# Block sums for both products of the second MoE, and sums between SBUF buffers on Pool

## The chip, the cores and the metric

The kernel runs on one core of a Trainium2 chip. The metric is the device time of one execution in microseconds. Engines are named as in the profile: PE (TensorE; PEld is its weight load), DVE (VectorE), ACT (ScalarE), POOL (GpSimd), SP (SyncE).

## What is computed

Three stages stand in a row: attention with a position bias, a first MoE that takes the largest of three products, and a second MoE with a gate.

```python
def _attn_ref(q, k, v, w1, b1, w2):
    ...
    scores = scores + bias.transpose(2, 0, 1)[None, :, :, :]
    ...
    return np.matmul(attn, v).astype(np.float32)

def _moe_ref(x, w1, w2, w3, w_out):
    h = np.maximum(np.maximum(x @ w1, x @ w2), x @ w3)
    return (h @ w_out).astype(np.float32)

def _moe2_ref(x, w_gate, w_val, w_out):
    gate = 1.0 / (1.0 + np.exp(-(x @ w_gate)))
    val = x @ w_val
    return (gate * val @ w_out).astype(np.float32)
```

Attention has 4 batches, 8 heads, 576 positions and 64 features a head. The MoEs see 2304 tokens of 512 features; the first has 768 inner columns and the second 1536.

## The kernel before

Every fp32 operand is split into two f16 halves (`hi` and `lo`), and a product is three matmuls for each 128 rows of the contraction: hi·hi, hi·lo, lo·hi. `halves` (line 1100) makes such a pair: ACT writes the scaled `hi`, DVE subtracts it from the scaled source and writes `lo`.

**The second MoE** works on one batch of 576 tokens after another. `quad(b, i)` makes 256 of the 1536 inner columns for batch b: six quads a batch, 24 in all. Its gate product is done by Strassen's scheme in Winograd's form: tokens and weights are cut in 2 x 2 blocks, seven sums of blocks are multiplied (seven groups of six matmuls of 128x288 each) and added up into four blocks of the result. DVE does this adding (lines 1279 to 1287), with one operand from PSUM and one from SBUF. The value product is plain: eight groups of six matmuls, left in two double PSUM banks (`two_r`). That makes 90 matmuls for a quad. ACT takes the gate's sigmoid (line 1298), DVE multiplies it with the value straight out of PSUM (line 1300), ACT casts the product to `hi` (line 1306), and DVE subtracts (`add2`, line 1096) to get `lo`.

**The block sums of the operands.** `token_sums(b, ...)` reads a batch's tokens back from DRAM, makes four sums (`add2`) and puts eight blocks into `XC`, which has two buffers, so the next batch's blocks can be made while the last one's are read (`next_tokens`). `pair_weights(i, ...)` makes the weights of a quad: DMA of 64-bit numbers, `decode64` (lines 554 to 556, integer steps on DVE), a sum of squares on ACT, a column sum on PE, then the scaled blocks; for the gate four `add2` sums come first. `out_weights(c, ...)` does the same for a quarter of the output weights, with the column scale at line 1208.

**Output matmuls.** `outs(pr, ct)` multiplies 128 finished tokens of batch pair `pr` with the output weights: 36 matmuls of 128x512 into bank 7 (later bank 4 too). The tables `after` and `ends` say behind which quads which of them are written: from quad (1,0) on, they stand between the quads.

**What sets the order.** All operations are recorded (`Recorder`), and `emit` deals them out to the engines by class and by modelled start time. The result is one fixed queue for each engine. An engine that waits for a semaphore holds everything behind it in its queue. `nc.join()` offers several engines for the same operation; `ADD_POOL`, which is off, would do that for `add2`.

Of the kernel before, what the change touches and what calls it, by code (L numbers as in the profile page):

```python
# [453 lines left out]
def tile_kernel(ctx, tc, q, k, v, w1, b1, w2, mw1, mw2, mw3, mwo, gw, vw, ow, xtab, masks, out):  # L454
# [725 lines left out]
    ob_m = X2[:, 3968:4992]  # L1180
# [3 lines left out]
    sg_r = Ring([sg_f, X2[:, 2816:3968]])  # L1184
# [68 lines left out]
    part_r, two_r = Ring([bank(i)[:, 0:HS] for i in (5, 6)]), Ring([bank(i, 1024).rearrange("p (a s) -> p a s", a=2)[:, :, 0:HS] for i in (0, 2)])  # L1253
    RAW = ((0, 1), (7, 2))

    def quad(b, i):
# [3 lines left out]
        sg, XC = sg_r(), XC_[b % 2]  # L1260
        c21, c22, c11, c12 = (sg[:, HS * n:HS * (n + 1)] for n in range(4))
# [3 lines left out]
        def group(ps, W, o, x, start, stop):  # L1265
            with nc.join():
                for kk in range(2):
                    for z, (wp, xp) in enumerate(((0, 0), (0, 1), (1, 0))):
                        nc.tensor.matmul(ps, lhsT=W[:, o, wp, kk], rhs=XC[:, x, xp, kk], start=start and kk == z == 0, stop=stop and kk == 1 and z == 2)  # L1269

        vs = []
        for t, n in enumerate((1, 6, 7, 5, 2, 3, 4)):
            ps = part_r()
            group(ps, SW[i][0], WS[n - 1], n - 1, True, True)
            with nc.at(BIAS):
                if n == 1:
                    copy_psum(c11, ps)
                elif n == 6:
                    nc.vector.tensor_tensor(c12, ps, c11, op=ALU.add)
                elif n == 7:  # L1280
                    nc.vector.tensor_tensor(c21, ps, c12, op=ALU.add)
                elif n == 5:
                    nc.vector.tensor_tensor(c12, ps, c12, op=ALU.add)
                    nc.vector.tensor_tensor(c22, ps, c21, op=ALU.add)
                else:
                    c = {2: c11, 3: c12, 4: c21}[n]
                    nc.vector.tensor_tensor(c, ps, c, op=ALU.add)  # L1287
            if t in (0, 2, 3, 5):
                m, hf = ((1, 0), (1, 1), (0, 0), (0, 1))[(0, 2, 3, 5).index(t)]
                if not hf:  # L1290
                    pv = two_r()
                    vs.append((m, pv))
                for kh in range(2):
                    group(pv[:, hf], SW[i][1], 2 * m + kh, RAW[hf][kh], kh == 0, kh == 1)
        with nc.at(BIAS):
            for m, pv in vs:
                at = sg[:, S * m:S * m + S]
                nc.scalar.activation(at, at, AF.Sigmoid, scale=ugm)  # L1298
                at = at.rearrange("p (a s) -> p a s", a=2)
# [69 lines left out]
    tx = [X2[:, 4992:5568], X2[:, 5568:6144]]

    def next_tokens(b):
        with nc.at(ATT):
            gx = gm_f[(1, 0, 1)[b]]
            token_sums(b + 1, gx[:, 0:1152], gx[:, 3072:4224], tx[b % 2])

    next_tokens(0)
# [47 lines left out]
```

## Time and profile before

| what | value |
|---|---|
| median of 3 runs | 1039.08 us (1037.2 to 1039.49) |
| the profiled execution's own time | 1040.86 us |
| span of its trace | 1039.1 us |
| granted PE clock, mean | 0.993 |
| PE busy | 993.7 us, 96% |
| DVE busy | 722.9 us, 70% |
| ACT busy | 597.6 us, 58% |
| POOL busy | 120.0 us, 12% |

The profile is one execution. Its page gives busy time by engine, the chain of work that ended last, and groups of instructions by line with their mean duration and with the idle time before them. The trace answers narrower questions: busy time in any stretch, an engine's timeline, the same groups with shapes kept apart. A line number there is one of the kernel printed above.

### The profile page before, as it was taken

The page shows a single profiled execution, that of the slowest core. Times are in us where ns is not written, and L with a number is a line of the kernel's source. Part 1 is how long each engine was busy: PE and PEld are TensorE (multiplying, and loading weights), DVE is VectorE, ACT ScalarE, POOL GpSimd, SP SyncE. Part 2 cuts the span into 40 slices and gives each one's busy share as a digit, 9 for nine tenths or more (in the row PEclk, how much of TensorE's full clock was granted, in tenths as well). Part 3 has the DMA queues.
Part 4 walks back from the last instruction along what each step waited for, and adds up shares of the span by engine and source line. Part 5 has one row for each costly group of instructions (what it writes and reads, how often), then busy time and mean ns, then how long its engine had stood idle before and what let it go on. Part 6 is the DMA issues. An engine that isn't in the chain of part 4 may idle for free.

```text
span 1039.1 us, 21298 instructions
## 1 busy us (share of the span) xinstructions
PE 993.7 (96%) x8156; PEld 670.1 (64%) x8156; DVE 722.9 (70%) x1869; ACT 597.6 (58%) x1336; POOL 120.0 (12%) x146
## 2 busy tenths in 40 slices
PE   4898999997999999999999999999999999999998
PEld 2344577664666666677677777876666656766653
DVE  5788998976878789958779989996354335532320
ACT  6898986775787777856765565653233124222221
POOL 1022114342112322112100100000000000000000
PEclk9999999998999999999999999999999999999999
DMA  7896767567999999875686233420010001000001
GB/s 222 252 303 226 271 211 174 164 165 143 213 228 261 234 219 250 206 199 128 146 181 188 82 104 116 138 62 11 11 67 11 11 11 66 2 11 22 11 11 41
DMA packets 172242, 139.49 MB, mean 134 GB/s; under 512 B 111852, under 2 KB 151020, under 8 KB 171628
## 3 DMA queue, kind: packets, MB, share of 16 engines
q1 hardware_dynamic: 169476, 128.39, 47.6%
q10 hardware_dynamic: 2664, 9.74, 3.3%
q8 instruction: 64, 1.05, 0.4%
q14 instruction: 38, 0.31, 0.1%
HBM read 94.25 MB, written 21.23 MB: 111 GB/s over the span
## 4 chain that ended last, share of the span: by engine, by line
PE 77%; DVE 9%; DMA 3%; issue 2%; ACT 2%; POOL 2%; SPq 0%; ACTq 0%; POOLq 0%; DVEq 0%
PE ps L1269 22%; PE ps L945 19%; PE ps L1325 13%; PE ps L890 7%; PE ps L831 5%; PE ps L863 5%; DMA am<-am 2%; PE ps L834 2%; PE ps L669 2%; POOL am L858 1%; DVE am L1103 1%; DVE am L847 1%; DVE wm L975 1%; PE ps L566 1%; PE ps L611 1%
## 5 line engine op out<-in xcount | busy, mean ns | idle before, releaser
L945 PE MATMUL ps<-wm 128*128 128x320 f16 (+2 forms) x2304 | 304.9, 286 | 0.2 <-DVE am L975 0.2
L945 PEld LDWEIGHTS <-wm 128*128 128x128 f16 x2304 | 222.9, 99 | 54.9 <-issue 3.2
L1269 PE MATMUL ps<-am 128*128 128x288 f16 x1800 | 223.9, 286 | 1.3 <-DVE wm L1300 0.7
L1269 PEld LDWEIGHTS <-am 128*128 128x128 f16 x1800 | 176.1, 98 | 48.5 <-issue 1.6
L1325 PE MATMUL ps<-wm 128*128 128x512 f16 x648 | 142.5, 379 | 0.0
L848 ACT ACTIVATE am<-am,small 128x576 f32<-128x576 f32 (+1 forms) x160 | 123.1, 770 | 30.3 <-DVE small L847 19.4
L847 DVE CUSTOM_DVE_ANT_0 am<-ps,am 128x576 f32<-128x576 f32 (+1 forms) x160 | 117.9, 749 | 28.2 <-issue 13.0
L1325 PEld LDWEIGHTS <-wm 128*128 128x128 f16 x648 | 63.3, 98 | 73.5
L858 POOL TENSOR_SCALAR am<-am,small 128x576 f32<-128x576 f32 (+1 forms) x65 | 64.5, 997 | 206.1 <-DVE small L850 135.5
L890 PE MATMUL ps<-am 128*64 128x128 f32 (+4 forms) x980 | 81.0, 313 | 1.1 <-DVE wm L896 0.7
L592 ACT ACTIVATE am<-ps 128x512 f32<-128x512 f32 (+3 forms) x146 | 66.1, 472 | 26.9 <-PE ps L863 23.5
L863 PE MATMUL ps<-ident,am 128*128 128x128 f32 x450 | 72.2, 282 | 7.5 <-POOL am L858 6.1
L863 PEld LDWEIGHTS ps<-ident,am 128*128 128x128 f32 x450 | 51.1, 143 | 26.1 <-POOL am L858 10.4
L1298 ACT ACTIVATE x<-x,ug 128x576 f32<-128x576 f32 x24 | 18.6, 775 | 77.8 <-DVE x L1287 77.7
L831 PE MATMUL ps<-am 64*128 64x512 f16 (+1 forms) x390 | 55.1, 384 | 7.3 <-DMA am<-am 6.8
L1333 ACT ACTIVATE x<-ps,uo 128x128 f32<-128x128 f32 x64 | 18.2, 368 | 75.3 <-PE ps L1325 55.4
L1298 ACT ACTIVATE wm<-wm,ug 128x576 f32<-128x576 f32 x24 | 18.5, 771 | 56.8 <-DVE wm L1287 56.8
L890 PEld LDWEIGHTS ps<-am 128*64 128x64 f32 x680 | 39.5, 137 | 17.8 <-issue 4.9
L872 DVE SCALAR_TENSOR_TENSOR am<-am,small 128x576 f16<-128x576 f32 (+1 forms) x60 | 48.0, 825 | 3.9 <-ACT am L871 3.8
L975 DVE SCALAR_TENSOR_TENSOR wm<-ps,small,wm 128x256 f32<-128x256 f32 (+1 forms) x84 | 43.0, 512 | 8.5 <-PE ps L945 6.8
L1269 PE MATMUL ps<-am,x 128*128 128x288 f16 x360 | 46.0, 286 | 2.5 <-DVE am L1103 1.9
L871 ACT ACTIVATE am<-am,small 128x576 f16<-128x576 f32 (+1 forms) x60 | 43.6, 766 | 5.3 <-ACT am L848 2.7
(180 smaller groups left out, 1382.6 us busy)
## 6 DMA issues: line engine op xcount, KB each, us to landing
am<-bias_d SPq DMA_DIRECT2D x49, 576.0 KB, 4.6
bias_d<-am SPq DMA_DIRECT2D x36, 320.0 KB, 4.4
wm<-in_moe_w_dram SPq DMA_DIRECT2D x12, 768.0 KB, 6.2
am<-bias_d ACTq DMA_DIRECT2D x15, 576.0 KB, 4.9
wm<-in_moe_w_out_dram SPq DMA_DIRECT2D x24, 256.0 KB, 2.9
x<-in_moe_w_val_dram SPq DMA_DIRECT2D x20, 256.0 KB, 4.1
x_d<-wm SPq DMA_DIRECT2D x4, 1152.0 KB, 4.7
am<-in_v_dram SPq DMA_DIRECT2D x16, 256.0 KB, 5.7
```

The lines of the kernel that those rows point to most:

```text
L592: nc.scalar.activation(dst, src, AF.Copy, scale=scale)
L831: nc.tensor.matmul(s_main[o][:m], lhsT=q_[h, eq], rhs=k_[h, ek, 0:512], start=(i == 0), stop=(i == 2), tile_position=(64 * o, 0))
L847: nc.vector.tensor_tensor_reduce(e[:m, c], S_[o][:m], bt[:m, c], -1.0, 3.0e38, ALU.add, ALU.min, mx[:m])
L848: nc.scalar.activation(e[:m, c], e[:m, c], AF.Exp, scale=-1.0, bias=mx[:m], accum_out=l[:m, o:o + 1])
L858: nc.gpsimd.tensor_scalar(e[:m, c], e[:m, c], r[:m, o:o + 1], 1.0, op0=ALU.mult, op1=ALU.mult)
L863: nc.tensor.transpose(ps[:, t], e[:, 128 * (t0 + t):128 * (t0 + t) + 128], ident)
L872: nc.vector.scalar_tensor_tensor(ph[:m, 1, c], e[:m, c], f, ph[:m, 0, c], op0=ALU.mult, op1=ALU.subtract)
L890: nc.tensor.matmul(ps[64 * o:64 * o + 64, :N], lhsT=vv[:, o, tv], rhs=pp[:, tb], start=(i == j == 0), stop=(i == len(todo) - 1 and j == 4) ...
L945: nc.tensor.matmul(ps, lhsT=W(wp, kk), rhs=X(xp, kk), start=(first and i == 0), stop=(last and i == 2))
L975: nc.vector.scalar_tensor_tensor(hv, ps, f, hv, op0=ALU.mult, op1=ALU.max)
L1269: nc.tensor.matmul(ps, lhsT=W[:, o, wp, kk], rhs=XC[:, x, xp, kk], start=start and kk == z == 0, stop=stop and kk == 1 and z == 2)
L1325: nc.tensor.matmul(po, lhsT=g[:, gi, kk], rhs=OW[:, wi, kk], start=(kk == 0 and i == 0), stop=(kk == K2 - 1 and i == 2))
```

## The change

The value product gets the same seven groups as the gate. A quad now makes its 14 groups in turn (gate, value, gate, ...), 84 matmuls in all, and every group lies in a single PSUM bank from a ring of six. The value's blocks are added up by DVE in SBUF (buffers from a new ring, `rp_r`), and the multiplication of gate and value (line 1291 of the changed kernel) reads both from SBUF.

The value's weights get four block sums and seven blocks, as the gate's have. `XC` holds seven blocks and only one batch: `token_sums(b + 1)` is written behind the quads of batch b.

`add2` is issued by Pool alone. It makes the sums of weight blocks (256 elements a row) and of token blocks (576). The `lo` half of the quads' products (1024 elements a row) is Pool's for batches 0 and 1 (`LO_POOL = 2`) and DVE's for batches 2 and 3; the two tails of 64 tokens stay on DVE. The `outs` are written at other places.

```diff
-ADD_POOL = False
+ADD_POOL = True
+LO_POOL = 2
...
-        with nc.join():
-            nc.vector.tensor_tensor(dst, a, b, op=op)
-            if ADD_POOL:
-                nc.gpsimd.tensor_tensor(dst, a, b, op=op)
+        (nc.gpsimd if ADD_POOL else nc.vector).tensor_tensor(dst, a, b, op=op)
...
-            W, s = SW[i][j], scl_gv[:, 0, i, j:j + 1]
-            if j:
-                for h in range(2):
-                    halves([W[:, 2 * h:2 * h + 2, e] for e in range(2)], f[:, :, 128 * h:128 * h + 128].rearrange("p (o k) f -> p o k f", o=2), s)
-                    yield
-                continue
-            t = S4().rearrange("p (o k f) -> p o k f", o=4, k=2)
+            W, s, t = SW[i][j], scl_gv[:, 0, i, j:j + 1], S4().rearrange("p (o k f) -> p o k f", o=4, k=2)
...
-    XC_ = [Am[:, 14080 + 4608 * i:18688 + 4608 * i].bitcast(F16).rearrange("p (o e k s) -> p o e k s", o=8, e=2, k=2) for i in range(2)]
+    XC = Am[:, 17920:21952].bitcast(F16).rearrange("p (o e k s) -> p o e k s", o=7, e=2, k=2)
...
-    part_r, two_r = Ring([bank(i)[:, 0:HS] for i in (5, 6)]), Ring([bank(i, 1024).rearrange("p (a s) -> p a s", a=2)[:, :, 0:HS] for i in (0, 2)])
-    RAW = ((0, 1), (7, 2))
+    part_r = Ring([bank(i)[:, 0:HS] for i in (0, 1, 2, 3, 5, 6)])
...
+        for n in (1, 6, 7, 5, 2, 3, 4):
+            for j in range(2):
+                c21, c22, c11, c12 = C[j]
+                ps = part(n, j)
+                with nc.at(BIAS):
+                    if n == 1:
+                        copy_psum(c11, ps)
+                    elif n == 6:
+                        nc.vector.tensor_tensor(c12, ps, c11, op=ALU.add)
...
-                nc.vector.scalar_tensor_tensor(at, pv, DOWN2, at, op0=ALU.mult, op1=ALU.mult)
+                nc.vector.scalar_tensor_tensor(sg[:, at], (r0, r1)[m], DOWN2, sg[:, at], op0=ALU.mult, op1=ALU.mult)
...
-                add2(lo, src, hi, ALU.subtract)
+                (nc.gpsimd if LO_POOL > b and src.shape[2] > 64 else nc.vector).tensor_tensor(lo, src, hi, op=ALU.subtract)
...
-    after = {0: {}, 1: {0: [0], 1: [1], 2: [2], 3: [3]}, 2: {0: [5], 1: [6], 2: [7], 3: [8]}, 3: {0: [0], 1: [1], 2: [2], 3: [3]}}
-    ends = {0: [], 1: [4], 2: [], 3: [4, 5, 6, 7, 8]}
...
+    after = {0: {}, 1: {1: [2], 3: [3]}, 2: {0: [6], 2: [7], 3: [8]}, 3: {1: [2], 3: [3]}}
+    ends = {0: [0, 1], 1: [4, 5], 2: [0, 1], 3: [4, 5, 6, 7, 8]}
...
+        if b < B - 1:
+            with nc.at(BIAS):
+                gx = gm_f[(1, 0, 1)[b]]
+                token_sums(b + 1, gx[:, 0:1152], gx[:, 3072:4224], gx[:, 1152:1728] if b else ob_m[:, 0:576])
```

How the queues change is read from the order of the instructions. Buffers there are `am`, `wm` and `x_75` (three large SBUF buffers) and `ps` (PSUM); the brackets name the engines or DMA lanes whose semaphores an instruction waits for.

PE, where the output matmuls first come. Before, behind all of quad (1,0) and 66 matmuls of quad (1,1):

```order
L1269 MATMUL ps<-am 128x288
L1269 LDWEIGHTS am
L1269 MATMUL ps<-am 128x288
L1325 LDWEIGHTS wm
L1325 MATMUL ps<-wm 128x512 [waits Activation_49]
L1325 LDWEIGHTS wm
L1325 MATMUL ps<-wm 128x512 [waits DVE_49]
```

In the changed kernel they come behind all quads of batches 0 and 1 but for 24 matmuls, and behind the column sum (line 567) of the last quarter of the output weights:

```order
L1261 MATMUL ps<-am 128x288
L1261 LDWEIGHTS am
L1261 MATMUL ps<-am 128x288
L567 MATMUL ps<-small,ones 128x6 [waits Activation_49]
L1316 LDWEIGHTS wm
L1316 MATMUL ps<-wm 128x512 [waits Activation_49]
L1316 LDWEIGHTS wm
L1316 MATMUL ps<-wm 128x512 [waits DVE_49]
L1316 LDWEIGHTS wm [waits Pool_49]
```

So 984 quad matmuls now stand ahead of the first output matmul, where 696 stood, and that one waits for DVE's, ACT's and Pool's share.

DVE in one of batch 0's quads. Before, with the decoding of output weights in between:

```order
L1281 TENSOR_TENSOR wm<-ps,wm 128x288 [waits DVE_49,PE_49]
L555 SCALAR_TENSOR_TENSOR wm<-wm 128x256 [waits DVE_49]
L554 TENSOR_SCALAR wm<-wm 128x256 [waits DMAHW5_49]
L556 SCALAR_TENSOR_TENSOR wm<-wm 128x256 [waits DVE_49]
L1283 TENSOR_TENSOR wm<-ps,wm 128x288 [waits PE_49]
L1284 TENSOR_TENSOR wm<-ps,wm 128x288
```

The same place in the changed kernel:

```order
L1275 TENSOR_TENSOR wm<-ps,wm 128x288 [waits DVE_49,PE_49]
L1275 TENSOR_TENSOR x_75<-ps,x_75 128x288 [waits DVE_49,PE_49]
L1101 SCALAR_TENSOR_TENSOR wm<-wm,small 128x2x128 [waits Activation_49]
L1282 TENSOR_TENSOR wm<-ps,wm 128x288 [waits DVE_49,PE_49]
L1283 TENSOR_TENSOR wm<-ps,wm 128x288
L1282 TENSOR_TENSOR x_75<-ps,x_75 128x288 [waits DVE_49,PE_49]
L1283 TENSOR_TENSOR x_75<-ps,x_75 128x288
```

Each sum out of PSUM now stands there twice, for the gate and for the value.

Pool behind the weights' sums, in batches 0 and 1, in the changed kernel (before, Pool had nothing at all to do here):

```order
L1096 TENSOR_TENSOR wm<-wm 128x2x288 [waits Pool_49]
L1298 TENSOR_TENSOR wm<-wm 128x1024 [waits PE_49,Activation_49]
L1298 TENSOR_TENSOR wm<-x_75,wm 128x1024 [waits PE_49,Activation_49]
L1298 TENSOR_TENSOR wm<-wm 128x1024 [waits PE_49,Activation_49]
L1298 TENSOR_TENSOR wm<-x_75,wm 128x1024 [waits Activation_49]
L1096 TENSOR_TENSOR wm<-wm 128x2x288 [waits DVE_49,Pool_49]
L1298 TENSOR_TENSOR wm<-wm 128x1024 [waits PE_49,Activation_49]
L1096 TENSOR_TENSOR wm<-wm 128x2x288 [waits DVE_49,Pool_49]
```

The low halves (line 1298) and the sums of the second batch's tokens (line 1096, 2x288) share one queue.

## Rows read from the trace of the kernel before

**Rows 1.** The page's first part: busy time, share and instructions of each engine.
```profile
PE 993.7 (96%) x8156; PEld 670.1 (64%) x8156; DVE 722.9 (70%) x1869; ACT 597.6 (58%) x1336; POOL 120.0 (12%) x146
```

**Rows 2.** Busy time in stretches of 20 us: PE, PEld, DVE, ACT, POOL, clock, DMA.
```profile
680.00:700.00 20.00, 17.84 (x146) 14.00 (x146) 19.90 (x49) 11.63 (x26) 0.00 (x0) 1.00 0.17 53
```

**Rows 3.** The same view of two longer stretches.
```profile
535.66:710.56 174.90, 168.44 (x1366) 132.70 (x1365) 162.75 (x443) 104.41 (x251) 5.00 (x3) 1.00 0.35 109
...
707.11:1034.50 327.39, 327.39 (x2181) 212.94 (x2179) 129.33 (x257) 87.60 (x179) 0.00 (x0) 1.00 0.06 22
```

**Rows 4.** PE's timeline: start, duration, line, tile, count, [idle before, releaser].
```profile
623.97 2.37 PE L1269 MATMUL ps<-am,x 128*128 128x288 f16 x18
...
694.47 3.22 PE L1269 MATMUL ps<-am,x 128*128 128x288 f16 x25 [0.26 <-DVE x L1300]
699.59 3.93 PE L1269 MATMUL ps<-am,x 128*128 128x288 f16 x29 [1.90 <-DVE am L1103]
703.86 1.82 PE L1269 MATMUL ps<-am,x 128*128 128x288 f16 x12 [0.34 <-DVE wm L1281]
706.23 0.90 PE L1269 MATMUL ps<-am 128*128 128x288 f16 x6 [0.55 <-DVE wm L1287]
```

**Rows 5.** The chain that ended last: start, duration, engine, line, count.
```profile
752.62 11.03 PE ps L1269 x90
763.65 7.77 PE ps L1325 x36
...
1028.02 6.62 issue
```

**Rows 6.** DVE's timeline in a quad of batch 1.
```profile
713.18 0.46 DVE L1283 TENSOR_TENSOR x<-ps,x 128x288 f32<-128x288 f32 x1
713.56 0.45 DVE L1284 TENSOR_TENSOR x<-ps,x 128x288 f32<-128x288 f32 x1
```

**Rows 7.** Groups by line and shape: count, busy us, mean ns, idle before.
```profile
L1300 DVE SCALAR_TENSOR_TENSOR wm<-ps,wm 128x576 f32<-128x576 f32 x24 | 18.1, 756 | 13.5 <-ACT wm L1298 13.4
L1287 DVE TENSOR_TENSOR wm<-ps,wm 128x288 f32<-128x288 f32 x36 | 16.4, 454 | 9.7 <-PE ps L1269 8.8
L1096 DVE TENSOR_TENSOR wm<-wm 128x1024 f16<-128x1024 f32 x12 | 14.6, 1220 | 6.0 <-ACT wm L1306 6.0
L1103 DVE SCALAR_TENSOR_TENSOR wm<-wm,small 128x256 f16<-128x256 f32 x24 | 10.3, 476 | 0.0
L1096 DVE TENSOR_TENSOR am<-am 128x256 f32<-128x256 f32 x16 | 6.0, 412 | 0.0
L1103 DVE SCALAR_TENSOR_TENSOR am<-am,gv_su 128x1024 f16<-128x1024 f32 x4 | 5.1, 1276 | 0.0
L1103 DVE SCALAR_TENSOR_TENSOR am<-am,gv_su 128x512 f16<-128x512 f32 x4 | 3.0, 750 | 0.1
```

**Rows 8.** POOL's timeline, its last three instructions before the quads.
```profile
560.20 1.28 POOL L986 TENSOR_TENSOR wm<-wm 128x576 f16<-128x576 f32 x1 [52.49 <-ACT wm L984]
578.57 1.69 POOL L986 TENSOR_TENSOR wm<-wm 128x576 f16<-128x576 f32 x1 [17.09 <-ACT wm L984]
589.29 2.03 POOL L986 TENSOR_TENSOR wm<-wm 128x576 f16<-128x576 f32 x1 [9.02 <-ACT wm L984]
```

**Rows 9.** DVE's timeline beside these, and a little before them.
```profile
560.69 1.14 DVE L554 TENSOR_SCALAR am<-am 128x256 int32<-128x256 int32 x2
...
577.97 0.48 DVE L554 TENSOR_SCALAR am<-am 128x256 int32<-128x256 int32 x2
578.38 0.75 DVE L555 SCALAR_TENSOR_TENSOR am<-am 128x256 int32<-128x256 int32 x2
...
579.18 1.70 DVE L556 SCALAR_TENSOR_TENSOR am<-am 128x256 int32<-128x256 int32 x2
...
589.76 0.42 DVE L556 SCALAR_TENSOR_TENSOR x<-x 128x256 int32<-128x256 int32 x1
590.10 0.47 DVE L975 SCALAR_TENSOR_TENSOR wm<-ps,small,wm 128x256 f32<-128x256 f32 x1
590.50 1.10 DVE L556 SCALAR_TENSOR_TENSOR x<-x 128x256 int32<-128x256 int32 x1
```

More of the change, by code (lines that the diff above doesn't have):

```diff
@@ L419 @@
 EARLY = 120
-ADD_POOL = False
+ADD_POOL = True
+LO_POOL = 2
 AHEAD = ()
-SPLIT5 = True
+SPLIT5 = False
 PE_ALL, PE_SQ = 6, 8
@@ L1075, in tile_kernel @@
     NP2 = K2 // 2
-    sw_d = {i: dram.tile([128, 2816], F32, tag=f"sw_d{i}", name=f"sw_d{i}") for i in AHEAD}
-    SW_f = [X2[:, 0:2816]] + [Am[:, 2816 * i:2816 * (i + 1)] for i in range(NP2 - 1)]
-    SW = [[t[:, a:a + 256 * n].bitcast(F16).rearrange("p (o e k f) -> p o e k f", o=n, e=2, k=2) for a, n in ((0, 7), (1792, 4))] for t in SW_f]
+    sw_d = {i: dram.tile([128, 3584], F32, tag=f"sw_d{i}", name=f"sw_d{i}") for i in AHEAD}
+    SW_f = [X2[:, 0:3584]] + [Am[:, 3584 * i:3584 * (i + 1)] for i in range(NP2 - 1)]
+    SW = [[t[:, 1792 * j:1792 * (j + 1)].bitcast(F16).rearrange("p (o e k f) -> p o e k f", o=7, e=2, k=2) for j in range(2)] for t in SW_f]
     WS = (0, 1, 6, 2, 3, 4, 5)
@@ L1177, in tile_kernel @@
                     moe1(b - 1, mm_b)
-    ob_m = X2[:, 3968:4992]
+    ob_m = Am[:, 21952:22976]
     gm_f, gt_f, ow_f, sg_f = [Wm[:, 6144:12288], Wm[:, 0:6144]], Wm[:, 12288:13824], Wm[:, 13824:19968], Wm[:, 19968:21120]
-    XC_ = [Am[:, 14080 + 4608 * i:18688 + 4608 * i].bitcast(F16).rearrange("p (o e k s) -> p o e k s", o=8, e=2, k=2) for i in range(2)]
+    XC = Am[:, 17920:21952].bitcast(F16).rearrange("p (o e k s) -> p o e k s", o=7, e=2, k=2)
     ob_r = Ring([ob_m[:, 512 * i:512 * (i + 1)] for i in range(2)])
-    sg_r = Ring([sg_f, X2[:, 2816:3968]])
+    sg_r = Ring([sg_f, X2[:, 3584:4736]])
+    rp_r = Ring([X2[:, 4736 + S * i:4736 + S * (i + 1)] for i in range(3)])
     gm = [t.bitcast(F16).rearrange("p (e k s) -> p e k s", e=2, k=K2) for t in gm_f]
@@ L1259, in quad, with part @@
         ugm = ug[:, b, i:i + 1]
-        sg, XC = sg_r(), XC_[b % 2]
-        c21, c22, c11, c12 = (sg[:, HS * n:HS * (n + 1)] for n in range(4))
+        sg = sg_r()
+        r1, r0 = rp_r(), rp_r()
+        C = [[t[:, HS * n:HS * (n + 1)] for t in x for n in range(2)] for x in ((sg[:, 0:S], sg[:, S:2 * S]), (r0, r1))]
         with nc.at(BIAS):
             nc.vector.tensor_scalar(ugm, scl["gw"][:, 1, i:i + 1], ub[:, b:b + 1], None, op0=ALU.mult)
-        def group(ps, W, o, x, start, stop):
+        def part(n, j):
+            ps = part_r()
             with nc.join():
@@ L1268, in group @@
                     for z, (wp, xp) in enumerate(((0, 0), (0, 1), (1, 0))):
[L1269 to L1294, printed above, removed]
@@ L1295, in quad @@
-        with nc.at(BIAS):
[L1296 to L1299, printed above, removed]
-                nc.vector.scalar_tensor_tensor(at, pv, DOWN2, at, op0=ALU.mult, op1=ALU.mult)
+                        nc.tensor.matmul(ps, lhsT=SW[i][j][:, WS[n - 1], wp, kk], rhs=XC[:, n - 1, xp, kk],
+                                         start=kk == z == 0, stop=kk == 1 and z == 2)
@@ new lines, in part @@
+            return ps
+        for n in (1, 6, 7, 5, 2, 3, 4):
[7 more added lines that the diff above has]
+                        nc.vector.tensor_tensor(c12, ps, c11, op=ALU.add)
+                    elif n == 7:
+                        nc.vector.tensor_tensor(c21, ps, c12, op=ALU.add)
+                    elif n == 5:
+                        if SPLIT5:
+                            copy_psum(c22, ps)
+                            add2(c12, c22, c12, ALU.add)
+                            add2(c22, c22, c21, ALU.add)
+                        else:
+                            nc.vector.tensor_tensor(c12, ps, c12, op=ALU.add)
+                            nc.vector.tensor_tensor(c22, ps, c21, op=ALU.add)
+                    else:
+                        c = {2: c11, 3: c12, 4: c21}[n]
+                        nc.vector.tensor_tensor(c, ps, c, op=ALU.add)
@@ L1301, in quad @@
+        with nc.at(BIAS):
+            for m in (1, 0):
+                at = slice(S * m, S * m + S)
+                nc.scalar.activation(sg[:, at], sg[:, at], AF.Sigmoid, scale=ugm)
+                nc.vector.scalar_tensor_tensor(sg[:, at], (r0, r1)[m], DOWN2, sg[:, at], op0=ALU.mult, op1=ALU.mult)
         g2 = sg.rearrange("p (m s) -> p m s", m=2)
@@ L1342, in tile_kernel @@
         pass
-    token_sums(0, Am[:, 18688:19840], Am[:, 19840:20992], Am[:, 20992:21568])
-    mems = parts(Am[:, 18688:22784], [1024, 1024, 512, 512, 512, 512]), parts(X2[:, 2816:6912], [1024, 1024, 512, 512, 512, 512])
+    token_sums(0, X2[:, 3584:4736], X2[:, 4736:5888], X2[:, 5888:6464])
+    mems = parts(Am[:, 14336:17920], [1024, 1024, 512, 512, 512]), parts(X2[:, 3584:6656], [1024, 1024, 512, 512])
     rings = [[Ring(m[2:]), Ring(m[0:1]), Ring(m[1:2])] for m in mems]
@@ L1366, in tile_kernel @@
     nc.cls = MOE
-    after = {0: {}, 1: {0: [0], 1: [1], 2: [2], 3: [3]}, 2: {0: [5], 1: [6], 2: [7], 3: [8]}, 3: {0: [0], 1: [1], 2: [2], 3: [3]}}
-    ends = {0: [], 1: [4], 2: [], 3: [4, 5, 6, 7, 8]}
[L1369 to L1376, printed above, removed]
+    after = {0: {}, 1: {1: [2], 3: [3]}, 2: {0: [6], 2: [7], 3: [8]}, 3: {1: [2], 3: [3]}}
+    ends = {0: [0, 1], 1: [4, 5], 2: [0, 1], 3: [4, 5, 6, 7, 8]}
     for b in range(B):
```

4 lines of the change are left out of this document (removed).

## The prediction

> **What bounds the kernel now.** I read the busy shares first: PE is busy for 993.7 us, 96% of the span, and DVE for 722.9, 70% [rows 1]. An average hides stages with different limits, so I cut the span into stretches of 20 us next. From 680 to 700, where the second MoE's first quads run, DVE is busy for 19.90 us and PE only for 17.84 [rows 2]. One longer stretch makes this exact: between attention's last DVE instruction (535.66) and the column scale of the last piece of the output weights (710.56) lie 174.90 us, with DVE busy for 162.75 and PE for 168.44; from 707.11 to 1034.50 PE has no idle time at all [rows 3], with the granted clock at 1.00, its upper level of 2.4 GHz, in all of it. So there are two regimes. Up to about 707 DVE and PE are nearly equally full and wait for each other; behind it PE alone sets the end. What is late at the seam is seen on PE's timeline: the first quad starts at 623.97, and at 694 to 707 PE waits 0.26, 1.90, 0.34 and 0.55 us for DVE, which is then making the second batch's token sums [rows 4]. The chain of waits gives the prices behind the seam: a quad's 90 matmuls take 11.03 us, 36 output matmuls 7.77, and the chain closes with 6.62 us of issue [rows 5]. From 1034.50, where PE really ends, to the span's end (1039.1) I count 4.6 us that the change leaves alone.
>
> **What is removed on PE.** A quad has 84 matmuls of 128x288 in place of 90, so 24 quads drop 144. One costs 11.03 / 90 = 0.1226 us, so PE loses 17.6 us of work, in a kernel that PE bounds for its last 327 us. If nothing else happened, the end would be 1039.1 - 17.6 = 1021.5.
>
> **What is added on DVE.** The value product was read straight out of PSUM by one multiplication; now its seven groups are summed like the gate's. Counting DVE's instructions between the same two places (attention's end, last column scale) in both programs gives the difference. That stretch now holds the sums of eleven and a half quads and not of seven, since no output matmul stands between them any more. A row lasts some 0.08 us longer than the distance to the next start (0.46 against 0.38 at 713.18 [rows 6]), so I take each mean of [rows 7] less 0.08. Added: 112 sums out of PSUM, 112 x 0.375 = 42.0; four more multiplications of 576, 2.8; five scalings of 1024, 6.0; nine of 256, 3.6; some twenty small ones, 2.7. Gone: five scalings of 512, 3.3; 20 weight sums of 256, 6.6; six token sums of 576, 4.0 (at the price of the 576 row); six low halves of 1024, 6.8. Together +36.4 us, so DVE's work from 535.66 on is 162.75 + 36.4 = 199.2, and it can't reach the last column scale before 734.8 even without a pause. Before, DVE paused for 12.15 us there. Blocks (below) fall partly into such pauses, so I keep half, 6: 740.8.
>
> **PE up to the same place.** The order puts all 984 quad matmuls of batches 0 and 1 ahead of the first output matmul: 623.97 + 984 x 0.1226 = 744.6, and some 3 us of pauses like those of [rows 4] make 747.6. So without any new wait, DVE (740.8) and PE (747.6) would arrive together. This is the thin point of the change: both engines lose their slack in the same 120 us. A delay on DVE goes to PE at once: six PSUM banks hold six groups, 6 x 6 x 0.1226 = 4.4 us of cover, and the sums that free them are queued behind whatever DVE is stuck in.
>
> **What follows behind it.** 24 leftover quad matmuls (2.9 us), 648 output matmuls at 7.77 / 36 = 0.2158 (139.8) and 1008 quad matmuls (123.5) are 266.3 us. I add 2.5 us for the two later changes of batch, 1.2 us from DVE's column scale to PE, and the 4.6 us tail. Had PE and DVE arrived at 747.6, the end would be 747.6 + 266.3 + 2.5 + 4.6 + about 1 = 1022. DVE was busy in only 129.33 of the last 327.39 us [rows 3], so the added sums of batches 2 and 3 (eight per quad, 8 x 0.375 = 3.0 us of DVE in 10.3 of PE) are covered and cost nothing.
>
> **What moves to Pool.** Sums with both operands in SBUF go to Pool alone: in the stretch, 40 weight sums of 256, eight token sums of 576, and low halves of 1024 (twelve, of which I count ten ahead of the first outputs); two of 576 stand there already. Pool's price is bounded by one kind of row, its 128x576 subtraction: 1.28 us at best, 1.69 and 2.03 in other places [rows 8]. By elements 256 costs 0.57 and 1024 2.28; the lower end is thus 40 x 0.57 + 10 x 1.28 + 10 x 2.28 = 58.4 us, the upper (1.28 for a sum of 256 too, which only a fixed cost would bring) 86.8. I take 58.4, since the row scales with what is moved. The Trainium skill, "GPSIMD Engine Reference", gives 4497 ns for an fp32 tensor_tensor add of 2048, which would make an estimate of 0.56 and 2.25 us; no run here shows it yet.
>
> Pool itself is mostly idle and could hide this. What speaks against it is DVE's timeline beside those Pool rows. While Pool's subtraction runs at 560.20, two DVE instructions that usually take 0.48 take 1.14; beside the one at 578.57 two that usually take 0.75 take 1.70; beside the one at 589.29 one takes 1.10 and not 0.42 [rows 8, 9]. That is 0.66, 0.95 and 0.68 us lost, 2.29 over Pool work that costs 3 x 1.28 = 3.84 clean: 60%. The DVE instruction that reads PSUM at 590.10 takes its usual 0.47 beside the same Pool row. So Pool's work is paid on DVE, by those instructions that take both operands from SBUF, and DVE has them everywhere here: the scalings, the integer steps that decode the weights' 64-bit numbers, and now also the multiplication of gate and value, which lost its PSUM operand. The Trainium skill, "SBUF — State Buffer", "Who interferes with whom", says that a DVE instruction with two SBUF inputs contends with a GpSimd instruction that reads SBUF, the second to come being blocked for the whole instruction; the trace agrees (1.10 against 0.42 us), and by that rule at its fullest all 58.4 us would be DVE's, which is the high rival below.
>
> **The forecast.** 60% of 58.4 is 35.0 us. DVE's last column scale: 740.8 + 35.0 = 775.8; PE starts the outputs at 777.0; the end is 777.0 + 266.3 + 2.5 + 4.6 = 1050.4. The moved sums save DVE 6.6 + 4.0 + 6.8 = 17.4 us (already in the 36.4) and cost it 35. Break-even is where the first outputs start at 1039.1 - 273.4 = 765.7, which is 23.7 us of blocking, 41% of Pool's time (17.7 us, 30%, if DVE keeps all 12.15 us of its pauses beside the blocks; with none of them 29.7, 51%). The profiled execution's span (1039.1) stands beside a median of 1039.08, so this sum needs no correction.
>
> **The rivals.**
> - *Pool hides (faster).* Where DVE reads PSUM it isn't blocked, and the quads add 112 such sums. With blocking of 0 to 30% (0 to 17.5 us) the end is 1022 to 1033. For it: Pool has the whole of each 10 us quad to find gaps. Against it: a Pool row of 2.28 us is longer than any gap, since a two-operand instruction follows within about a microsecond on DVE. Up to 1037: 0.27.
> - *It cancels.* By the rule just quoted blocking follows the share of two-operand work on DVE. From counts and the same prices this is some three quarters ahead of the quads and 40% in them. With 60% there (of 28 us of Pool) and 30% in the quads (of 30) it is 26 us, and the end 1041. Between 1037 and 1041: 0.10.
> - *Slower still.* Every Pool microsecond is paid: 58.4, an end of 1073.8. Or the token blocks, now in one buffer, can't be overwritten until the last quad of a batch has read them; PE would wait for 7 scalings (0.73 each, 5.1 us) at each of three changes of batch less the 2.5 counted, another 5 to 10 us: 1055 to 1060. Over 1058: 0.17.
> - *The forecast,* 1041 to 1058: 0.46.
>
> A measurement of this kernel can tell about 0.2% from no change, so "same" is 1037.0 to 1041.2. Faster is then 0.27, same 0.10, slower 0.63. The range goes from 1025 (blocking near 15%, under which I leave 0.08) to 1068 (blocking near 90%, above which I leave 0.12).
>
> **What would show it.** On the after trace: (1) quads of 84 matmuls in about 10.3 us where PE is undisturbed. (2) Pool's 1024 rows near 2.28 us and its sums of 256 near 0.57. (3) DVE rows with two SBUF operands stretched by a microsecond or more beside Pool rows, sums out of PSUM not. (4) The first output matmul near 777, PE with some 30 us of pauses between 624 and 777, released by DVE. (5) PE full behind it. It would be wrong if the first output matmul starts near 750 (Pool hidden), or if PE has long pauses behind 777, which my sum doesn't contain, or if Pool rows take twice the price.

## The result: slower by about 1%

The changed kernel takes 1052.2 us in the median (1042.2 to 1064.8, 20 runs) against 1041.6 of the kernel before; the ratio is 1.008, with a 95% interval of 1.005 to 1.011. Forecast were 1050 and "slower". Five of the changed kernel's 20 runs, over 1.5% above its fastest, are left out of the ratio; the other 15 have a median of 1049.6. A second set of runs gave 1.0125 (1.009 to 1.016). Single executions of the changed kernel differ by up to 2.2%, in good part ahead of the second MoE: attention's last DVE instruction came between 526 and 543 us in the traces of this document. So I compare traces from that instruction on, and times by the ratios.

The two measures don't agree fully. In the six traces with the changed kernel's order (the changed kernel twice, e1 to e4 below) attention's last DVE instruction comes at 533 us in the mean, in six with the old order ahead of the first output matmul (before, e5 to e7, f1 and f2) at 539. Behind it the changed kernel is 15.1 us later than the kernel before (518.5 against 503.4), while the ratios say 0.8 to 1.25%, 8 to 13 us. Something seems to shorten the part ahead of it by some 6 us; single traces of one order lie up to 13 us apart, and the cause was not looked for.

The page's first part of the changed kernel (busy us, share, instructions), to set beside [rows 1]:

```profile
PE 990.0 (94%) x8012; PEld 661.7 (63%) x8012; DVE 797.2 (75%) x1989; ACT 609.1 (58%) x1362; POOL 212.5 (20%) x220
```

PE has its 144 matmuls less, yet it was busy for only 3.7 us less; DVE has 74.3 us more and POOL 92.5. The rows from here on are of a second profiled execution of the same kernel (the run a0_again below); the first has the same lengths within 1.1 us. Busy time from attention's last DVE instruction to the first quad, from there to the first output matmul, and behind it (columns as in [rows 2]):

```profile
537.31:636.79 99.48, 91.73 (x738) 71.59 (x737) 87.92 (x206) 58.11 (x148) 38.82 (x42) 1.00 0.40 122
636.79:783.17 146.38, 128.86 (x999) 99.19 (x997) 139.88 (x349) 69.06 (x150) 26.41 (x13) 0.96 0.17 53
783.17:1044.00 260.83, 260.83 (x1648) 161.44 (x1648) 131.93 (x261) 75.88 (x162) 18.59 (x11) 0.99 0.08 26
```

Beside [rows 3], three things are to be seen. The first output matmul comes 245.9 us behind attention's end. DVE is busy for 227.8 of these, PE for 220.6. And behind 783.17 PE has no pause at all. So nearly all of the loss stands ahead of the first output matmul. PE's pauses in the quads, from its timeline (start, duration, tile, count, [idle before, what ended it]):

```profile
646.99 1.60 PE L1261 MATMUL ps<-am 128*128 128x288 f16 x6 [3.68 <-DVE wm L1286]
...
698.70 0.39 PE L567 MATMUL ps<-small,ones 128*128 128x6 f32 x2 [1.93 <-ACT junk L1197]
714.68 10.52 PE L1261 MATMUL ps<-am,x 128*128 128x288 f16 x71 [2.96 <-DVE am L1101]
751.16 0.39 PE L567 MATMUL ps<-small,ones 128*128 128x6 f32 x2 [1.97 <-ACT junk L1197]
779.81 0.39 PE L567 MATMUL ps<-small,ones 128*128 128x6 f32 x2 [1.58 <-ACT junk L1197]
783.17 9.55 PE L1316 MATMUL ps<-wm 128*128 128x512 f16 x36 [2.97 <-ACT wm L1100]
```

The pause at 714.68 is the change from batch 0 to 1, where the tokens' blocks can't be made earlier any more. Those on line 567 are column sums of the output weights, which wait for ACT, and ACT for DVE's decoding. The last one is the first output matmul itself, behind the last quarter of the output weights.

What DVE is held up by, from POOL's and DVE's timelines at two quads' ends:

```profile
656.53 2.23 POOL L1298 TENSOR_TENSOR wm<-wm 128x1024 f16<-128x1024 f32 x1 [11.77 <-ACT wm L1297]
667.64 2.13 POOL L1298 TENSOR_TENSOR wm<-x,wm 128x1024 f16<-128x1024 f32 x1 [8.88 <-PE ps L1261]
```
```profile
656.69 2.22 DVE L1298 TENSOR_TENSOR wm<-wm 128x128 f16<-128x128 f32 x1
...
668.06 1.85 DVE L1298 TENSOR_TENSOR wm<-x,wm 128x128 f16<-128x128 f32 x1
```

The 128-element subtraction on DVE (the tail of 64 tokens) takes 0.28 us where Pool is idle. It stands right behind the cast that releases Pool's subtraction of 1024, and lasts nearly as long as that one. Summed over all DVE instructions that overlap one of Pool's and last longer than their kind does elsewhere, it is 8.9 us ahead of the quads and 17.7 in them, 26.6 together. Such a sum depends by 1 to 3 us on what is taken as the usual length. I call it DVE's standing still.

### The profile page after: what moved, and what is told of

Read it like the earlier page. It is cut to its first block, busy times and chain, and to the rows that moved or that the text cites. A ratio compares the mean times of both kernels' runs of the same rounds, so it can differ in the third digit from the quotient of the medians.

```text
span 1056.7 us, 21435 instructions
## 1 busy us (share of the span) xinstructions
PE 990.0 (94%) x8012; PEld 661.7 (63%) x8012; DVE 797.2 (75%) x1989; ACT 609.1 (58%) x1362; POOL 212.5 (20%) x220
## 5 line engine op out<-in xcount | busy, mean ns | idle before, releaser
L1261 PE MATMUL ps<-am 128*128 128x288 f16 x1680 | 211.5, 288 | 5.0 <-DVE wm L1286 3.6
L1261 PEld LDWEIGHTS <-am 128*128 128x128 f16 x1680 | 165.3, 99 | 50.1 <-issue 6.3
L832 PE MATMUL ps<-am 64*128 64x512 f16 (+1 forms) x390 | 57.3, 391 | 8.1 <-DMA am<-am 5.2
L1324 ACT ACTIVATE am<-ps,uo 128x128 f32<-128x128 f32 x64 | 18.3, 368 | 77.9 <-issue 49.5
L1290 ACT ACTIVATE wm<-wm,ug 128x576 f32<-128x576 f32 x24 | 18.6, 774 | 68.3 <-DVE wm L1286 65.2
L1286 DVE TENSOR_TENSOR x<-ps,x 128x288 f32<-128x288 f32 x108 | 47.4, 449 | 13.0 <-PE ps L1261 13.0
L873 DVE SCALAR_TENSOR_TENSOR am<-am,small 128x576 f16<-128x576 f32 (+1 forms) x60 | 50.6, 869 | 4.4 <-ACT am L872 2.8
L772 POOL TENSOR_SCALAR am<-am,small 128x320 f16<-128x320 f32 x48 | 31.1, 663 | 93.3 <-DVE small L767 78.3
```

Of the source, the lines that this page charges most:

```text
L832: nc.tensor.matmul(s_main[o][:m], lhsT=q_[h, eq], rhs=k_[h, ek, 0:512], start=(i == 0), stop=(i == 2), tile_position=(64 * o, 0))
L873: nc.vector.scalar_tensor_tensor(ph[:m, 1, c], e[:m, c], f, ph[:m, 0, c], op0=ALU.mult, op1=ALU.subtract)
L1261: nc.tensor.matmul(ps, lhsT=SW[i][j][:, WS[n - 1], wp, kk], rhs=XC[:, n - 1, xp, kk], start=kk == z == 0, stop=kk == 1 and z == 2)
```

## The experiments

Three theories are weighed: L (the lock), W (work) and, from the fifth run on, S (stage); the texts on record say what each is.

Three lengths make the runs comparable: from attention's end to the first quad, from there to the first output matmul, and the rest of the span. All are in us and come from one profiled execution each; the ratios are of the timed runs. Fields are empty where output matmuls stand between the quads.

| run | to first quad | to first output | rest | all behind attention | ratio to before (95%) |
|---|---|---|---|---|---|
| before | 88.3 | (outputs between quads) | | 503.4 | 1 |
| changed (a0_again) | 99.5 | 146.4 | 272.6 | 518.5 | 1.0125 (1.0088 to 1.0162) |
| e4_tail_pool | 98.2 | 145.7 | 273.3 | 517.2 | 1.0093 (1.0057 to 1.0129) |
| e1_sums_dve | 90.7 | 152.3 | 273.2 | 516.1 | 1.0111 (1.0078 to 1.0144) |
| e2_lo_dve | 98.5 | 146.3 | 272.6 | 517.4 | 1.0125 (1.0079 to 1.0171) |
| e3_all_dve | 90.5 | 148.2 | 272.7 | 511.4 | 1.0028 (0.9998 to 1.0059) |
| e5_pool_reads | 88.0 | | | 516.7 | 1.0186 (1.0140 to 1.0232) |
| e6_pool_writes | 88.3 | | | 503.9 | 0.9990 (0.9954 to 1.0025) |
| e7_pool_reads_late | 88.3 | | | 504.1 | 1.0002 (0.9970 to 1.0033) |
| f1_late | 88.1 | | | 494.4 | 0.9907 (0.9870 to 0.9943) |
| f2_late_pool | 87.8 | | | 495.1 | 0.9943 (0.9908 to 0.9978) |

### The changed kernel and four ways to give Pool less or more

The edits of e1 to e4 are against the changed kernel. `emit` then deals all operations out anew, so the order changes too: with the two queues lined up, 50 to 360 of PE's 8012 matmuls stand elsewhere in these four. A microsecond or two between them can come from the order as well.

> The changed kernel once more, so that the three beside it have their own reference. In its first trace 36 DVE instructions last longer beside Pool instructions than elsewhere, by 25.4 us together: 8.7 ahead of the quads and 16.6 in them. Theory L (the lock): this is what turned a gain of 17.6 us into a loss. Rival W (work): the loss is the 36 us of sums that DVE got on top, in an order that puts no output matmul between the quads of batches 0 and 1; Pool's part is hidden. Both expect 1046 to 1055 us here, first output matmul 240 to 247 us behind attention's last DVE instruction.

1052.1 us, 245.9 us to the first output matmul, 26.6 us of DVE's standing still.

```diff
-                (nc.gpsimd if LO_POOL > b and src.shape[2] > 64 else nc.vector).tensor_tensor(lo, src, hi, op=ALU.subtract)
+                (nc.gpsimd if LO_POOL > b else nc.vector).tensor_tensor(lo, src, hi, op=ALU.subtract)
```

> Only the low halves of the 64-token tails of batches 0 and 1 move too, from DVE to Pool. On DVE each stands right behind the cast that also starts Pool's subtraction of 1024, and lasts 1.9 to 2.2 us in the trace where 0.28 is usual; that is 11.4 of the 16.6 us. L expects the first output matmul about 10 us earlier and the end 8 to 12 us earlier than the changed kernel's. W expects 12 x 0.2 = 2.4 us of DVE work less, an end 0 to 3 us earlier.

L missed: the first output comes 243.9 us behind attention's end, 2.0 earlier, and the median is 1049.6, 2.6 earlier, in W's range. The reason is in the trace. The tails are gone from DVE, but other instructions are now stretched in their stead. Groups on DVE in the quads (mean ns is the number behind the busy time):

```profile
L1101 DVE SCALAR_TENSOR_TENSOR wm<-wm,small 128x256 f16<-128x256 f32 x19 | 11.9, 635 | 0.8 <-ACT wm L1100 0.8
...
L1101 DVE SCALAR_TENSOR_TENSOR am<-wm,small,am 128x576 f16<-128x576 f32 x6 | 6.6, 1118 | 0.1
L1101 DVE SCALAR_TENSOR_TENSOR am<-am,small 128x576 f16<-128x576 f32 x1 | 2.4, 2395 | 0.0
```

The scaling of 256 takes 476 ns in the kernel before [rows 7], the one of 576 some 810. By the same count DVE stands still for 13.3 us in the quads, and not for 17.7 - 11.3 = 6.4. In this trace the stops moved to other instructions that read SBUF, above all to the scalings and the decoding.

```diff
-ADD_POOL = True
+ADD_POOL = False
```

> All sums of weight and token blocks go back to DVE (40 of 256 and 8 of 576 in the stage, 40 x 0.33 + 8 x 0.67 = 18.6 us of DVE work); the low halves of 1024 stay on Pool. L expects that the 8.7 us ahead of the quads, some 4 us beside the token sums and some 4 us of waits for Pool go, so the end is 0 to 4 us later than the changed kernel's. W expects it 15 to 19 us later.

L's range (0 to 4 us later) is met within the scatter: 1051.2 us, 0.9 earlier than the changed kernel. W, which expected 15 to 19 later, missed. The way there is another than I thought: the stage ahead of the quads is 8.8 us shorter, and the quads take 5.9 us longer, with 15.3 us of standing still beside the low halves.

```diff
-LO_POOL = 2
+LO_POOL = 0
```

> The low halves of 1024 go back to DVE (ten ahead of the first outputs, 10 x 1.14 = 11.4 us); the sums of blocks stay on Pool. L expects that some 13 of the 16.6 us in the quads go, so the end is between 3 us earlier and 1 us later than the changed kernel's. W expects it 9 to 12 us later.

L's range again (1050.4 us, 1.7 earlier), and W missed again. DVE's standing still in the quads fell from 17.7 to about 4 us, and the work it got instead (nine low halves, some 10 us) and 2.4 us more of pauses ate that up: the quads take 146.3 us as before. PE now runs through its quads and waits at the end for the output weights (PE's timeline):

```profile
767.52 0.59 PE L567 MATMUL ps<-small,ones 128*128 128x6 f32 x2 [12.30 <-ACT junk L1197]
771.10 3.24 PE L1316 MATMUL ps<-wm 128*128 128x512 f16 x7 [2.98 <-ACT wm L1100]
```

So up to the first output matmul it seems to be DVE's queue that has to be finished, and PE's pauses only move within it.

```diff
-ADD_POOL = True
-LO_POOL = 2
+ADD_POOL = False
+LO_POOL = 0
```

> Pool gets none of the moved work: the sums of blocks and the low halves are all DVE's again, the rest is as in the changed kernel. The three runs before this one gave new numbers: from attention's last DVE instruction to the first output matmul 245.9 us in the changed kernel, 243.9 with the tails on Pool, 243.0 with the sums on DVE, 244.8 with the low halves on DVE. So a fourth theory, S (stage): up to the first output matmul DVE is the bound, and whatever it is spared by Pool it pays back by standing still. By S this run has 26.6 us of standing still less and 18.6 + 11.4 us of work more, so 245 to 251 us and an end 0 to 5 us later than the changed kernel's. By L in its first form (the standing still is the whole loss) the stage would be 15 us or more shorter.

S missed, in its direction too: it expected an end 0 to 5 us later. With nothing moved to Pool the kernel is at 1.0028, which is 5 to 10 us faster than the changed one by its two ratios and 7.1 by the traces, and 238.7 us to the first output are below the 245 expected. L in its first form (15 us or more) got about half of what it expected:

```profile
529.71:620.23 90.52, 88.21 (x720) 69.62 (x718) 87.01 (x235) 56.21 (x146) 8.53 (x5) 1.00 0.44 133
620.23:768.38 148.15, 125.05 (x998) 98.40 (x996) 137.17 (x367) 70.02 (x150) 0.00 (x0) 0.93 0.17 52
```

DVE is busy for 224.2 us, less than in the changed kernel (227.8), although it does some 20 us more of work: 40 sums of 256, four of 576 and nine low halves are its own again, while four of the first MoE's subtractions fewer stand on it there. It also pauses less, 14.5 us against 18.1. Moving either part back alone (e1, e2) brought 1 to 2 us, both together 7; with one part left on Pool DVE still stands still for about 20 us (e1) and over 10 (e2). That splits the loss behind attention in two: Pool's part is 7.1 us of the 15.1, and without it the kernel still ends 8.0 us later behind attention than before (511.4 against 503.4), though by the ratio of the whole only 0.3% (0.0 to 0.6). So PE's 17.6 us are used up without Pool already. Whether by the value's sums on DVE or by what else the change did to the order (no output matmuls between these quads, one token buffer) was not tried apart.

### The lock by itself

The kernel before gets 12 instructions on Pool whose results nobody uses. No other engine's queue changes: PE, DVE and ACT have the same instructions in the same order in both traces.

```diff
                 add2(lo, src, hi, ALU.subtract)
+                if b < 2 and src.shape[2] > 64:
+                    nc.gpsimd.tensor_tensor(extra, src, hi, op=ALU.subtract)
```

> The kernel before with extra work on Pool: behind each quad's low half in batches 0 and 1 Pool repeats the same subtraction of 1024 into a buffer that nobody reads (12 instructions, 2.13 us each; nothing else changes its place in any queue). It measures the lock by itself. If Pool's reads of SBUF stop DVE: about half a dozen of them fall ahead of 710 us where DVE is full, each costs DVE 1 to 2 us, and PE's pauses there grow; the end is 4 to 12 us later than before. If Pool were free: 0 to 1 us.

More than expected (4 to 12 us): 1059.0 us, 17.6 above the median of before in the same set, and 13.3 behind attention in the trace. In the quads up to the first output matmul, where seven of the subtractions stand, DVE's rows beside Pool are 13.3 us longer than their kinds elsewhere: here the whole of it reached the end. What the other 4 us of the medians are, the trace doesn't show. The other kind, fills in place of subtractions:

```diff
                 add2(lo, src, hi, ALU.subtract)
+                if b < 2 and src.shape[2] > 64:
+                    nc.scalar.copy(extra[:, 0:1], src[:, 0, 0:1])
+                    for _ in range(3):
+                        nc.gpsimd.memset(extra, 0.0)
```

> The same kernel before with Pool as long busy at the same places, but with instructions that only write SBUF: three fills of 768 elements in place of each subtraction, released by a one-element copy on ACT. If what stops DVE is the two engines' reading of SBUF, DVE's rows keep their usual lengths and the end is within 2 us of before. If any work on Pool stops DVE, it is as late as with the subtractions.

No difference in time: 0.9990 (0.9954 to 1.0025). The queues of PE and DVE are again those of the kernel before; ACT has the 12 copies more. The first of these places in both traces, POOL and then DVE; with subtractions:

```profile
641.08 3.17 POOL L1310 TENSOR_TENSOR x<-wm 128x1024 f16<-128x1024 f32 x1 [48.54 <-ACT wm L1307]
```
```profile
641.04 3.36 DVE L1096 TENSOR_TENSOR wm<-wm 128x1024 f16<-128x1024 f32 x2 [0.41 <-ACT wm L1307]
```

And with fills:

```profile
645.39 2.33 POOL L1312 MEMSET x<- 128x768 f32 x3 [49.57 <-ACT x L1310]
```
```profile
645.27 1.43 DVE L1096 TENSOR_TENSOR wm<-wm 128x1024 f16<-128x1024 f32 x2 [0.41 <-ACT wm L1307]
```

The same two DVE instructions take 3.36 and 1.43 us, with Pool busy beside both. Pool's own subtraction takes 3.17 here and 2.13 where DVE leaves it alone, which fits that it first waits for DVE's subtraction of 1024 and that DVE's tail then waits for it. In the group of tails over the quads up to the first output, first with subtractions, then with fills:

```profile
L1096 DVE TENSOR_TENSOR wm<-wm 128x128 f16<-128x128 f32 x4 | 6.9, 1734 | 0.0
```
```profile
L1096 DVE TENSOR_TENSOR wm<-wm 128x128 f16<-128x128 f32 x4 | 1.1, 285 | 0.0
```

A Pool instruction that reads SBUF stops these DVE instructions and one that only writes it doesn't, as the Trainium skill says in "SBUF — State Buffer", "Who interferes with whom"; the trace agrees (1734 against 285 ns).

The fills are not free for all of DVE, though. The decoding's first step (line 554), which reads a single operand from SBUF, takes 0.28 us as a rule, and longer beside them:

```profile
678.71 0.28 DVE L554 TENSOR_SCALAR wm<-wm 128x256 int32<-128x256 int32 x1
...
703.00 0.59 DVE L554 TENSOR_SCALAR wm<-wm 128x256 int32<-128x256 int32 x1
```

Pool's fills run from 701.11 to 703.44. In the seven quads up to the first output this is 1.2 us in all, too little to show at the end.

The subtractions once more, in batches 2 and 3 (the edit is against e5):

```diff
-                if b < 2 and src.shape[2] > 64:
+                if b >= 2 and src.shape[2] > 64:
                     nc.gpsimd.tensor_tensor(extra, src, hi, op=ALU.subtract)
```

> The kernel before with the same extra subtractions on Pool as in the run where they stood in batches 0 and 1 (there the end came 1.9% later), now in batches 2 and 3 instead. DVE was busy in some 40% of that stage. If a stop of DVE costs only where DVE is the bound, the end is within 2 us of before, though DVE's rows beside Pool's are as long as there. If every stop of DVE reaches the end, it is 10 us or more later.

No difference (1.0002, 0.997 to 1.003), though DVE's rows there are stretched as well:

```profile
L1096 DVE TENSOR_TENSOR wm<-x,wm 128x128 f16<-128x128 f32 x9 | 12.2, 1357 | 0.0
L1096 DVE TENSOR_TENSOR wm<-wm 128x128 f16<-128x128 f32 x8 | 10.0, 1250 | 0.0
```

DVE loses some 23 us in that stage, and PE pauses for 0.32 us in it. What a stop costs is decided by the stage, not by the stop.

### Block sums only where PE is the bound

From that a version follows: the kernel before, with the value's block sums in batches 2 and 3 alone. Batches 0 and 1 keep the plain product, and nothing goes to Pool. Some output matmuls of batches 2 and 3 are written at other places. The four sums of the value's weights are made on DVE at the end of batch 1 and in batch 2, out of the two f16 halves that already lie in SBUF, into the token buffer that batch 1 has left (`XC` has one buffer from then on).

```diff
+    def late_sums(i):
+        V = SW[i][1]
+        nc.vector.tensor_tensor(scr, V[:, :, 0], V[:, :, 1], op=ALU.add)
+        a21, a22, a11, a12 = (scr[:, o] for o in range(4))
+        nc.vector.tensor_tensor(a22, a21, a22, op=ALU.add)
+        nc.vector.tensor_tensor(a21, a11, a21, op=ALU.subtract)
+        nc.vector.tensor_tensor(a11, a22, a11, op=ALU.subtract)
+        nc.vector.tensor_tensor(a12, a12, a11, op=ALU.subtract)
...
-    ends = {0: [], 1: [4], 2: [], 3: [4, 5, 6, 7, 8]}
...
+    ends = {0: [], 1: [4, 5], 2: [0, 1], 3: [4, 5, 6, 7, 8]}
...
-            quad(b, i)
+            (quad if b < LATE else quad_late)(b, i)
```

> The kernel before with the value product by block sums in batches 2 and 3 alone, where DVE was busy in 129 of 327 us, and with nothing moved to Pool. The missing sums of the value's weights are made on DVE in batch 2 out of the two f16 halves that lie in SBUF. 12 quads x 6 matmuls x 0.1226 = 8.8 us of PE less; DVE gets about 23 us for the weights and 12 x 3 for the value's sums, all in the stage that PE bounds. By S the end is 5 to 9 us earlier than before (ratio 0.991 to 0.995). If the value's sums cost by themselves, wherever they stand, it is later than before.

1030.4 us, a ratio of 0.991 (0.987 to 0.994), as S expected: faster than both kernels, and than e3 (1.003), which has the same sums in all batches. Behind attention it takes 494.4 us, 9.0 less than before, where 72 matmuls are worth 8.8. From the first output matmul to 1025 PE has no pause, and DVE is busy for 174 of 310 us:

```profile
714.59:1025.00 310.41, 310.41 (x2042) 199.21 (x2039) 173.82 (x357) 93.61 (x190) 0.00 (x0) 1.00 0.07 23
```

Its low halves of batches 2 and 3 on Pool (against f1):

```diff
     def quad_late(b, i):
...
-                add2(lo, src, hi, ALU.subtract)
+                nc.gpsimd.tensor_tensor(lo, src, hi, op=ALU.subtract)
```

> The kernel with the value's block sums in batches 2 and 3 alone, with the low halves of these two batches moved from DVE to Pool. DVE is spared 12 x (1.14 + 0.20) = 16 us in a stage that PE bounds. If DVE has slack there, neither the work that is spared nor the standing still is seen: an end within 2 us of the same kernel without the move (1030.4), or up to 3 us later through the last quad's low half, which 36 output matmuls wait for.

1035.7 us in another set of runs, 0.9943 (0.9908 to 0.9978), by the ratios 3.7 us later than f1 where at most 3 were expected; the intervals of the two versions overlap. Behind attention the trace shows 0.7 us more, which is this one pause of PE for Pool:

```profile
907.41 8.81 PE L1391 MATMUL ps<-wm 128*128 128x512 f16 x40 [0.84 <-POOL wm L1320]
```

So there is no gain in relieving DVE where it has slack, and a wait for Pool's longer instruction can show at the end. Whether the other 3 us between the ratios are more than scatter, these runs can't tell.

## Why the prediction was right, step by step

- **PE's saving.** Right: 8156 matmuls became 8012, and a quad of 84 takes 10.29 us where PE is undisturbed (forecast 10.3).
- **DVE's added work.** Right: 227.8 us busy less 26.6 of standing still is 201.2; forecast were 199.2. Single counts were off and nearly cancel: eight multiplications came on top and not four, four scalings of 576 fell away that the sum leaves out, and eight token sums had stood there, not six.
- **Both engines arrive together.** Right: 241.3 us were forecast from attention's end to the first output matmul, 244.6 and 245.9 measured. DVE was busy for 93% of this stretch and PE for 90%, so stops of DVE went on to PE (the pauses by DVE and ACT above).
- **Pool's price.** Near for the low halves (2.13 us where undisturbed, forecast 2.28), too low for the small sums: three of 256 take 2.09 us in a row, 0.70 each, against 0.57. As an estimate, 0.70 for 256 and 2.13 for 1024 leave some 0.2 us that doesn't grow with the elements, which scaling left out. Four token sums and nine low halves stood in the stretch, where eight and ten were counted.
- **The lock.** Right in kind (e5, e6), too large in size: 35 us were forecast and 26.6 counted, of Pool's 65 us busy there 41% and not 60%. The rate was not the same everywhere: 23% ahead of the quads (8.9 of 38.8 us), beside sums of 256, and 67% in them (17.7 of 26.4), beside the long low halves. The three rows on which 60% rests stand beside subtractions of 576. One of them is not what it was taken for: line 554, at 560.69 [rows 9], reads a single operand from SBUF. In the changed kernel such a step is stretched too, POOL and then DVE:

```profile
728.34 2.65 POOL L1298 TENSOR_TENSOR wm<-wm 128x1024 f16<-128x1024 f32 x1 [9.39 <-ACT wm L1297]
```
```profile
729.64 1.49 DVE L555 TENSOR_SCALAR wm<-wm 128x256 int32<-128x256 int32 x1
```

  So "both operands from SBUF" is not the whole condition, though most of the standing still lies on such instructions.
- **DVE's pauses.** Too small: 6 forecast, 18.1 measured. The trace puts 8.0 us of them to PE, 4.5 to ACT, 2.1 to DMA and none to Pool; 14.5 are left in e3, without the moved work. So 41 us of stops and pauses were forecast and 44.7 came: the two errors nearly cancel, and the time is closer than its terms deserve. The end is lucky in a second way: behind attention 514.7 us were forecast and 517 to 518.5 came, 2 to 4 more, and the median is still within 2 us of the forecast. The part ahead, which the forecast takes at 535.66, lies between 526 and 540 us in the six traces with the changed order.
- **What the move to Pool costs in all.** This is the step that was mis-sized. The prediction set 35 us of stops against 17.4 us of saved work, net 17.6. But the 17.4 counted six low halves, as many as DVE made in that stretch before; the changed kernel would make ten, so the work saved is 18.6 + 11.4 = 30 us (the sum for the whole was not touched by this). With that, the prediction's own terms give for the kernel without Pool's part 740.8 + 30.0 + 1.2 + 273.4 = 1045.4; e3 measured 1043.9. With the counts of the trace (40 sums, four and nine) the work saved is 26 us, and the same terms give 1041.6. The net price of the move is 5 or 9 us by these terms, and 5 to 10 by the ratios.
- **Change of batch.** One pause of 2.96 us at the first; none at the two later ones, for which I had 2.5 us.
- **Behind the first output.** 273.4 us forecast, 272.6 measured. The 2.5 us for the batches did not come; 1.8 us of slower output matmuls (below) did.
- **The rivals.** "Pool hides" fell with e5: Pool's reading is paid on DVE even where nobody waits for Pool. "It cancels" gave 1041 and fell with the ratio; it set the higher rate ahead of the quads and the lower one in them, and the count shows the reverse. "Slower still" fell too; no pause is seen at the later changes of batch.

## To carry to other kernels

A saving on the engine that bounds the end is worth nothing in a stage where another engine is as full and gets the work. Cut the span into stages, make the exchange only where the receiving engine has slack (here 0.991, where all batches gave 1.003, and 1.008 with Pool's part), and check the queue up to the first consumer. Pool isn't a free second vector engine: where it reads SBUF, DVE's instructions with two SBUF operands pay for it, and so did a one-operand step here. Moving the one that is hit let others be hit (e4).

## What the runs showed of the hardware that was not expected

**A pause of PE costs twice.** Behind each of the longer pauses of the quads the matmuls run slower for a while. The granted clock (the third number from the end of a row) in stretches of 4 us around the ends of three pauses:

```profile
646.00:650.00 4.00, 3.02 (x14) 1.88 (x14) 3.28 (x8) 2.38 (x5) 0.00 (x0) 0.57 0.23 66
650.00:654.00 4.00, 4.00 (x35) 3.19 (x33) 3.53 (x10) 1.60 (x3) 0.00 (x0) 1.00 0.02 4
714.00:718.00 4.00, 3.32 (x15) 2.07 (x15) 4.00 (x6) 1.57 (x4) 1.55 (x1) 0.59 0.01 2
...
783.00:787.00 4.00, 3.83 (x11) 1.34 (x11) 3.85 (x6) 2.11 (x6) 2.09 (x1) 0.58 0.00 0
787.00:791.00 4.00, 4.00 (x20) 1.80 (x19) 1.41 (x3) 0.41 (x1) 2.35 (x2) 1.00 0.00 0
```

PE had idled for 3.68, 2.96 and 2.97 us. A mean of 0.57 to 0.59 is mostly the lower of the two levels (1.2 of 2.4 GHz). The 36 output matmuls at 783.17 took 9.55 us where 7.77 is usual. Over the quads 128.86 us of PE were spent on 984 matmuls that cost 120.6 at the upper level, and on 12 column sums; the mean clock of 0.96 over these 146 us makes 5 to 6 us of the difference (an estimate). Behind the shorter pauses of the kernel before (up to 1.90 us, [rows 4]) the clock stayed at 1.00 [rows 3]. Two pauses in these quads that are nearly as long as that differ, 1.93 us at 698.70 and 1.97 at 751.16; the stretches behind them:

```profile
698.00:702.00 4.00, 3.30 (x27) 2.69 (x28) 3.24 (x10) 2.76 (x7) 0.00 (x0) 1.00 0.20 66
752.00:756.00 4.00, 4.00 (x21) 2.57 (x19) 3.69 (x9) 0.64 (x3) 2.12 (x1) 0.57 0.01 5
```

**The two engines take turns.** Where sums of 256 stand in a row on Pool and integer steps on DVE, both are stretched; from DVE's and POOL's timelines of the changed kernel:

```profile
576.94 0.57 DVE L556 SCALAR_TENSOR_TENSOR am<-am 128x256 int32<-128x256 int32 x1
577.55 0.83 DVE L557 SCALAR_TENSOR_TENSOR am<-am 128x256 int32<-128x256 int32 x1
```
```profile
543.91 2.09 POOL L1096 TENSOR_TENSOR am<-am 128x256 f32<-128x256 f32 x3 [0.91 <-DVE am L557]
...
576.50 2.46 POOL L1096 TENSOR_TENSOR x<-x 128x256 f32<-128x256 f32 x3 [2.51 <-DVE x L557]
```

Three sums take 2.09 us at best and 2.46 here, an integer step 0.83 and not 0.42. Ahead of the quads, where Pool's sums are small, DVE lost 8.9 us over 38.8 us of Pool; in the quads, with the low halves of 1024, it lost 17.7 over 26.4. Whether it is the length of Pool's instructions or DVE's place in its queue that makes the second rate higher was not tried.
